# Token sums on GpSimd instead of TensorE, two more row buffers, and a changed first and last step in a two-part attention kernel

## The chip, the cores and the metric

The kernel runs on one core of one Trainium2 chip. The metric is the device time of one execution in microseconds, as the median of several runs.

## The reference

Two attention blocks work on separate inputs of 2048 tokens and 640 features, with 32 heads of 20 features each; their outputs stand side by side in one array of 2048 x 1280, in bf16.

```python
def _A_ref(x, wqkv, wo):          # H = 32, Dh = 20, W = 256
    q, k, v = split_heads(x @ wqkv)
    scores = einsum("bhqd,bhkd->bhqk", q, k) * Dh ** -0.5
    mask = (i - j >= 0) & (i - j < W)
    p = softmax(where(mask, scores, -1e9))
    return heads_joined(einsum("bhqk,bhkd->bhqd", p, v)) @ wo

def _B_ref(x, wqkv, wo):
    q, k, v = split_heads(x @ wqkv)
    phi = lambda t: where(t > 0, t + 1, exp(t)) + 1e-6
    pq, pk = phi(q), phi(k)
    kv = einsum("bhsd,bhse->bhde", pk, v)
    z = einsum("bhsd->bhd", pk)                       # sum over all tokens
    num = einsum("bhqd,bhde->bhqe", pq, kv)
    den = einsum("bhqd,bhd->bhq", pq, z)[..., None] + 1e-6
    return heads_joined(num / den) @ wo
```

A is sliding-window attention, B is linear attention. The vector z, the sum of the keys' features over the tokens, is what the change works on most.

## The kernel before

The tokens are worked in four tiles of 512 (t = 0 to 3), of four blocks of 128 rows each. One function, `build`, first lists operations: each has its engine or engines, its dependencies, and the buffers that it takes and gives back. The order in which they are then written out is a fixed list, `SEQ`: each number is an operation times eight plus an engine, so the list also says which of ScalarE (ACT) and VectorE (DVE) makes an eviction. Every engine executes its own instructions strictly in this order, and so do the queues of DMA issues on SP, ACT and POOL. Where an engine has to wait, all that is behind it on that engine waits too.

Part A. `proj` makes q and k of a tile (line 577), and `proj_v` makes v (line 638). Heads that lie badly for TensorE's row groups are moved to another tile, `odd`, by DMAs issued on POOL (lines 608 and 611), called relays here. `attn` makes scores in one PSUM buffer S (line 708), ACT takes the exponentials (line 724), DVE multiplies the window's edges by 0 or 1 (line 736, the masks, a product of two inputs in SBUF), and TensorE multiplies p by v (line 764). `a_out` divides and multiplies by the output weights (line 798).

Part B. `b_keys` makes pk = phi(k) for all 16 blocks of rows (line 913; ACT and DVE finish it in lines 874 to 881); pk of a tile of 512 tokens lies in SBUF under the tags K0 to K3. `b_sums` makes G, the product of B's input and pk over all tokens (line 938). `b_z` sums pk over the tokens: 32 matmuls with a matrix of ones (line 974) into two PSUM buffers, which DVE splits into a bf16 part and its rest (lines 986 and 989, z.hi and z.lo), ten matmuls with one column that turn the sum into a column (line 995), and on DVE the block pattern Zc (line 1002). `b_kvwo` multiplies G by the value weights and the output weights (lines 1037 and 1055). `b_query` makes pq (line 1107) and the denominators (line 1125), divides (line 1171), and multiplies by the matrix of `b_kvwo` (line 798 again).

`finish_rows` makes one block of 128 output rows: two groups of five matmuls of 320 columns each, an eviction of each into a row buffer (`osb`, lines 484 on ACT and 486 on DVE), and one store of the row (line 812). The row buffers are four slots, O0 to O3:

```python
pl = Planner(FB + ["S0"] + [f"O{i}" for i in range(PRM.get("nosb", 4))] + ["L0"])
```

A slot is taken by the first eviction of a row and given back when the store has landed. The products of line 1055 are evicted into the same slots.

PSUM for all but the scores is four buffers, F0 to F3. At the start PE runs matmuls on a tile of zeros, `warm`, that DVE fills first (line 504, matmuls of line 1185); x of the first 128-row blocks is loaded, turned by TensorE (line 1242) and copied out; and the value weights arrive in five blocks of 128 rows, three on ACT's queue and two on SP's.

Of the kernel before, what the change touches and what calls it, by code (L numbers as in the profile page):

```python
# [14 lines left out]
PRM = {"sq": "SP", "dens": 4}  # L15
TUNE = {}
SEQ = [
# [372 lines left out]
def build(nc, pools, A_x, A_wqkv, A_wo, B_x, B_wqkv, B_wo, out):  # L390
# [6 lines left out]
    NQ = 512  # L397
    NTT = 4
    HALF = 320
    WIDE = bool(PRM.get("wide"))  # L400
    SWD = 640 if WIDE else 512
    scale = float(Dh) ** -0.5
    NF = 3 if WIDE else 4
# [1079 lines left out]
```

## Time and profile before

| | us |
|---|---|
| median of 3 runs | 250.51 (250.25 to 251.5) |
| the profiled execution, its own time | 250.49 |
| its span, first to last instruction | 248.8 |
| PE busy | 239.9 |
| ACT busy | 200.8 |
| DVE busy | 172.6 |
| POOL busy | 40.4 |

The span is one execution's time from the first to the last instruction; the execution's own time also holds what lies around it. PE is TensorE's matmuls, PEld its weight loads, DVE VectorE, ACT ScalarE, POOL GpSimd, SP SyncE. In a row of a group, the numbers behind the bars are busy us, mean ns of one, and idle us of the engine before it with what ended the idle time. In the chain and the timeline a row starts with its start and its length in us.

### The profile page before, as it was taken

What the parts mean: (1) busy time and instruction counts of PE and PEld (TensorE: products, weight loads), DVE (VectorE), ACT (ScalarE), POOL (GpSimd) and SP (SyncE); (2) the same over time, 40 slices, a digit from 0 to 9 for tenths busy, and PEclk for the clock granted to TensorE, in tenths of its full rate; (3) what the DMA queues carried; (4) which work ended last, traced back from release to release, by engine and by line L of the source; (5) the groups of instructions that cost most, each with busy time, mean ns of one, the idle gap of its engine ahead of it and who ended that gap; (6) DMA issues with size and microseconds to landing.
All of it is one profiled execution on the core that took longest, in us unless ns stands there. A gap on an engine that the chain in (4) does not pass through costs nothing.

```text
span 248.8 us, 9643 instructions
## 1 busy us (share of the span) xinstructions
PE 239.9 (96%) x4167; PEld 144.3 (58%) x4193; DVE 172.6 (69%) x441; ACT 200.8 (81%) x222; POOL 40.4 (16%) x93
## 2 busy tenths in 40 slices
PE   7999999999999999999999999999989999999993
PEld 6644565454655666545566666666555665565671
DVE  2553587778679978886666363369999899949740
ACT  2459898988999999988998788789999987946532
POOL 6003460063002601004078000000000000000000
PEclk9999999999999999999999999999999999999999
DMA  6999226649364759913573768863545472236433
GB/s 216 284 148 243 59 66 148 154 90 166 87 223 111 198 99 213 277 42 72 143 194 75 124 154 258 202 164 105 159 139 151 119 167 84 76 114 186 135 128 111
DMA packets 54216, 36.61 MB, mean 147 GB/s; under 512 B 34249, under 2 KB 52761, under 8 KB 54169
## 3 DMA queue, kind: packets, MB, share of 16 engines
q1 hardware_dynamic: 50537, 31.52, 49.7%
q0 software_dynamic: 2048, 2.63, 5.3%
q10 hardware_dynamic: 1584, 1.80, 2.2%
q8 instruction: 33, 0.54, 1.0%
q14 instruction: 14, 0.11, 0.2%
HBM read 13.90 MB, written 10.26 MB: 97 GB/s over the span
## 4 chain that ended last, share of the span: by engine, by line
PE 87%; ACT 6%; DVE 3%; issue 2%; DMA 1%; ACTq 0%; DVEq 0%
PE F L577 17%; PE F L798 16%; PE S L708 10%; PE F L638 9%; PE F L913 9%; PE F L938 9%; PE F L764 6%; PE F L1107 5%; ACT p L724 4%; DMA out_dram<-osb 1%; PE F L1185 1%; DVE pq L881 1%; PE F L1037 1%; ACT e L874 1%; PE F L1242 1%
## 5 line engine op out<-in xcount | busy, mean ns | idle before, releaser
L724 ACT ACTIVATE p<-S 128x2048 bf16<-128x2048 f32 x76 | 141.1, 1856 | 16.4 <-PE S L708 14.5
L736 DVE TENSOR_TENSOR p<-p,strip 128x256 bf16<-128x256 bf16 (+2 forms) x140 | 49.4, 381 | 21.1 <-ACT p L724 20.5
L874 ACT ACTIVATE e<-F 128x320 bf16<-128x320 f32 (+1 forms) x52 | 25.5, 501 | 8.3 <-PE F L1107 5.8
L638 PE MATMUL F<-wv,xT 128*128 128x320 bf16 x160 | 31.7, 300 | 0.1
L913 PE MATMUL F<-wkB,xT 128*128 128x320 bf16 x160 | 30.7, 299 | 0.2 <-issue 0.2
L798 PE MATMUL F<-woA,oc 128*128 128x320 bf16 x160 | 30.3, 300 | 0.0
L611 POOL DMA_DIRECT2D odd<-st x32 | 18.2, 573 | 69.3 <-ACT st L484 28.8
L577 PE MATMUL F<-xT,wk 128*128 128x512 bf16 x91 | 27.8, 380 | 0.3
L577 PE MATMUL F<-xT,wq 128*128 128x512 bf16 x92 | 26.9, 380 | 0.5 <-issue 0.3
L938 PE MATMUL F<-pk,xtok 128*128 128x320 bf16 x160 | 27.1, 300 | 0.0
L798 PE MATMUL F<-kvwo,pq 128*128 128x320 bf16 x160 | 25.9, 300 | 0.9 <-DVE pq L1171 0.4
L1107 PE MATMUL F<-xT,wqB 128*128 128x512 bf16 x91 | 25.4, 381 | 0.3
L486 DVE CAST ost<-F 128x512 bf16<-128x512 f32 x26 | 17.1, 685 | 10.2 <-PE F L764 10.0
L486 DVE CAST even<-F 128x512 bf16<-128x512 f32 x24 | 16.5, 688 | 8.2 <-PE F L577 7.9
L486 DVE CAST osb<-F 128x320 bf16<-128x320 f32 x33 | 15.5, 486 | 8.6 <-PE F L798 7.9
L608 POOL DMA_DIRECT2D odd<-even x32 | 16.6, 524 | 25.4 <-DVE even L486 23.2
L764 PE MATMUL F<-p,vt 64*32 64x320 bf16 (+4 forms) x720 | 20.5, 253 | 0.0
L638 PEld LDWEIGHTS <-xT 128*128 128x128 bf16 x160 | 15.1, 98 | 9.2 <-issue 1.3
L913 PEld LDWEIGHTS <-xT 128*128 128x128 bf16 x160 | 15.0, 98 | 8.9 <-issue 1.2
L764 PE MATMUL F<-p,sw 64*32 64x320 bf16 (+3 forms) x720 | 19.9, 253 | 0.2 <-DVE kvs L486 0.2
L798 PEld LDWEIGHTS <-pq 128*128 128x128 bf16 x160 | 14.9, 98 | 8.7 <-issue 1.6
L484 ACT CAST osb<-F 128x320 bf16<-128x320 f32 x31 | 12.6, 426 | 8.5 <-PE F L798 6.2
(85 smaller groups left out, 295.8 us busy)
## 6 DMA issues: line engine op xcount, KB each, us to landing
OD<-ost SPq DMA_DIRECT2D x32, 128.0 KB, 2.2
out_dram<-osb SPq DMA_DIRECT2D x24, 160.0 KB, 2.1
oc<-OD SPq DMA_DIRECT2D x4, 640.0 KB, 4.9
xtok<-in_B_x_dram SPq DMA_DIRECT2D x4, 640.0 KB, 4.5
odd<-even POOLq DMA_DIRECT2D x32, 48.0 KB, 2.9
sw<-vt SPq DMA_DIRECT2D x16, 87.0 KB, 3.1
out_dram<-osb ACTq DMA_DIRECT2D x8, 160.0 KB, 2.1
odd<-st POOLq DMA_DIRECT2D x32, 32.0 KB, 3.1
```

Source lines behind the costliest of these rows:

```text
L486: nc.vector.tensor_copy(out=dst, in_=src)
L577: nc.tensor.matmul(ps[:, a:b], lhsT=w[:, kt, i, :], rhs=xb["t"][:, kt, a:b], start=(kt == 0), stop=(kt == KT - 1))
L638: return lambda ps: nc.tensor.matmul(ps[:], lhsT=xb["t"][:, kt, bb * P : bb * P + P], rhs=rhs_(), start=(kt == 0), stop=(kt == KT - 1))
L708: nc.tensor.matmul(st["s"][64 * i : 64 * i + 64, o0 : o0 + b - a], lhsT=kb["t"][32 * j : 32 * j + Dh, sl, ko : ko + 64], rhs=qb["t"][32 * ...
L724: nc.scalar.activation(out=o_, in_=i_, func=ACT.Exp, scale=scale)
L736: nc.vector.tensor_tensor(out=x, in0=x, in1=mkv[:, None, :].to_broadcast([P, 4, 64 * w]), op=ALU.mult)
L764: nc.tensor.matmul(O[i][32 * j : 32 * j + 32, a:b], lhsT=lhsT, rhs=pb["t"][64 * i : 64 * i + 64, o0 + js * j : o0 + js * j + b - a], start ...
L798: return lambda ps: nc.tensor.matmul(ps[:], lhsT=lhs(c), rhs=rhs(c, hf), start=(c == 0), stop=(c == KT - 1))
L874: nc.scalar.activation(out=eb["t"][:, 0:n], in_=ps[:], func=ACT.Exp)
L913: return lambda ps: nc.tensor.matmul(ps[:], lhsT=xb["t"][:, kt, b * P : (b + 1) * P], rhs=R["wkB"][:, kt, hf * HALF : (hf + 1) * HALF], st ...
L938: return lambda ps: nc.tensor.matmul(ps[:], lhsT=R["xt", tb // 4][:, tb % 4, c * P : (c + 1) * P], rhs=R["pk", tb // 4][:, tb % 4, hf * HA ...
L1107: return lambda ps: nc.tensor.matmul(ps[:], lhsT=R["wqB"][:, kt, :].rearrange("p (f c) -> p c f", c=KT)[:, c, :], rhs=xb["t"][:, kt, :], s ...
```

## The change

- The sums of line 974 go. Fifteen GpSimd additions of 128 x 640 sum the 16 blocks of pk into a float32 tile, `zacc`. What follows (z.hi, z.lo) reads this tile instead of PSUM, in one instruction of 640 columns each instead of two of 320. The ten one-column matmuls then take a column of ones.
- Two more row slots, OK2 and OK3, lie over pk of tiles 2 and 3. They are held from the start and given free by z.hi and z.lo, when pk is no longer needed.
- The last block of rows of B (`ob3.3`) is made in three groups, of 320, 160 and 160 columns, and stored in two parts, of 480 and 160 columns.
- The warm-up matmuls read a constant of ones that the framework fills ahead of all engines' work, and there are 22 instead of 20 (beside 8 others that are the same in both).
- Block 0 of the value weights is the first, not the second, on ACT's queue. This and all else that is only order comes with a new list `SEQ`, which also gives some evictions to the other engine.
- Six rounds of four matmuls of 8 columns stand ahead of the first denominator. In the first tile, p times v goes through its pieces in another order.

In the new order the additions stand on POOL behind twelve of the sixteen relays of the last tile and ahead of the other four. The last group of all is one of 160 columns (columns 320 to 480), evicted by ACT, and the store of 480 columns, issued by ACT, is the last.

The diff, without `SEQ` and without paths that the settings leave off:

```diff
-PRM = {"sq": "SP", "dens": 4}
+PRM = {"sq": "SP", "dens": 4, "zs": "POOL", "xo": 1, "dpad": 6, "lastb": 3, "nwarm": 22}
...
+    XO = {"OK2": "K2", "OK3": "K3"} if PRM.get("xo", 1) else {}
+    pl = Planner(FB + ["S0"] + list(XO) + [f"O{i}" for i in range(PRM.get("nosb", 4))] + ["L0"])
+    held = [{} for _ in XO]
+    for g_ in held:
+        pl.op({"SP": 1}, lambda e: None, -(10 ** 8), [], name="hold", slots=(1, "O"), g=g_)
...
-        warm = mk("o", [P, NQ], BF16, "warm", tag="L0")
-        nc.vector.memset(warm[:], 0.0)
+        warm = nc.const_aps.tensor(1.0, (P, P), BF16)
...
+    def row_tile(sb, name):
+        tag = sb["slot"][0]
+        return mk("over", [P, D], BF16, name, tag=XO[tag]) if tag in XO else mk("o", [P, D], BF16, name, tag="osb" + tag)
+
-    def finish_rows(tb, col0, lhs, rhs, key, deps, name):
+    def finish_rows(tb, col0, lhs, rhs, key, deps, name, last=False):
...
-        for hf in range(2):
+        cuts = [(0, HALF), (HALF, 480), (480, D)] if last else [(0, HALF), (HALF, D)]
+        for k, (a, b) in enumerate(cuts):
...
-        st = dma(lambda e: q_of(e).dma_start(out=out2[tb * P : (tb + 1) * P, col0 : col0 + D], in_=sb["t"][:]), D_STORE, -4000, ends, name="store")
+        for a, b, need in [(0, 480, ends[:2]), (480, D, ends[2:])] if last else [(0, D, ends)]:
+            st = dma(lambda e, a=a, b=b: q_of(e).dma_start(out=out2[tb * P : (tb + 1) * P, col0 + a : col0 + b], in_=sb["t"][:, a:b]), (340, 1, int(420 * (b - a) / D), 350), -4000, need, name="store")
...
+            for k in range(1, NT):
+
+                def add(e, k=k):
+                    if "zacc" not in R:
+                        R["zacc"] = mk("const", [P, D], F32, "zacc")
+                    blk = lambda i: R["pk", i // 4][:, i % 4, :]
+                    (nc.vector if ZS == "DVE" else nc.gpsimd).tensor_tensor(out=R["zacc"][:], in0=blk(0) if k == 1 else R["zacc"][:], in1=blk(k), op=ALU.add)
+
+                need = pk_ops[2 * k : 2 * k + 2] + (pk_ops[0:2] if k == 1 else [prev])
+                prev = pl.op({ZS: {"DVE": 820, "POOL": 1500}[ZS]}, add, 4000 + k, need, name=f"zs{k}")
...
+            a = pl.op({"DVE": 490 if one else dve_ps(HALF)}, hi, EVK, need, name="z.hi", rel=[(g_, 0) for g_ in (held[0:1] if one else held[k : k + 1])])
+            evs.append(pl.op({"DVE": 820 if one else dve_ps(HALF)}, lo, EVK, [a], name="z.lo", rel=rel + [(g_, 0) for g_ in (held[1:2] if one else [])]))
...
+                for i in range(PRM.get("dpad", 0) if t == 0 else 0):
+                    for s_ in range(4):
+                        nc.tensor.matmul(dg["w"][32 * s_ : 32 * s_ + 32, 256:264], lhsT=ones[:], rhs=ones[:, 0:8], start=True, stop=True, tile_position=(0, 32 * s_), skip_group_check=True)
...
-                nc.tensor.matmul(psum(g)[:, 0:P], lhsT=warm[:, 0:P], rhs=warm[:, 0:P], start=True, stop=True)
+                nc.tensor.matmul(psum(g)[:, 0:P], lhsT=warm[:, 0:P], rhs=warm, start=True, stop=True)
```

More of the change, by code (lines that the diff above doesn't have):

```diff
@@ L502, in build @@
     if not dry:
-        warm = mk("o", [P, NQ], BF16, "warm", tag="L0")
-        nc.vector.memset(warm[:], 0.0)
-        nc.scalar.preload_act_table_set("natural_log_exp_and_others")
+        warm = nc.const_aps.tensor(1.0, (P, P), BF16)
+        if not XT0:
+            nc.scalar.preload_act_table_set("natural_log_exp_and_others")
         tiny = mk("const", [P, 1], F32, "tiny")
         nc.vector.memset(tiny[:], 1e-6)
-        tinyo = mk("const", [P, 1], F32, "tinyo")
-        nc.scalar.activation(out=tinyo[:], in_=tiny[:], func=ACT.Exp)
+        if not XT0:
+            tinyo = mk("const", [P, 1], F32, "tinyo")
+            nc.scalar.activation(out=tinyo[:], in_=tiny[:], func=ACT.Exp)
         ident = mk("const", [P, P], BF16, "ident")
@@ L576, in m @@
                     w = wq if which == "q" else wk
-                    nc.tensor.matmul(ps[:, a:b], lhsT=w[:, kt, i, :], rhs=xb["t"][:, kt, a:b], start=(kt == 0), stop=(kt == KT - 1))
+                    rhs = xb["t"][:, :, kt, :] if t == 0 and XT0 else xb["t"][:, kt, a:b]
+                    nc.tensor.matmul(ps[:, a:b], lhsT=w[:, kt, i, :], rhs=rhs, start=(kt == 0), stop=(kt == KT - 1))
                 return m
@@ L637, in mm @@
                         rhs_ = lambda: wv[:, kt, :].rearrange("p (a i n) -> p a i n", a=2, i=2)[:, :, i, :]
+                        if t == 0 and XT0:
+                            return lambda ps: nc.tensor.matmul(ps[:], lhsT=xb["t"][:, bb, kt, :], rhs=rhs_(), start=(kt == 0), stop=(kt == KT - 1))
                         return lambda ps: nc.tensor.matmul(ps[:], lhsT=xb["t"][:, kt, bb * P : bb * P + P], rhs=rhs_(), start=(kt == 0), stop=(kt == KT - 1))
@@ L966, in b_z @@
         R["cst"] = co
-        zg = {}
-        def emz(e):
-            ps = [psum(zg, hf, [P, HALF]) for hf in range(2)]
-            for b in range(4):
-                for hf in range(2):
-                    for s in range(4):
-                        nc.tensor.matmul(ps[hf][32 * s : 32 * s + 32, :], lhsT=ones[:], rhs=R["pk", s][:, b, hf * HALF : (hf + 1) * HALF], start=(b == 0), stop=(b == 3), tile_position=(0, 32 * s), skip_group_check=True)
         R["gm"] = gm = list(g_mm)
-        zo = pl.op({"PE": 1120}, emz, kv("z", key), [pk_ops, gm], mode="z", slots=(2, "F"), g=zg, name="z", cls="Z", ni=64)
@@ L978, in b_z, with emz @@
         hl = {}
+        ZS = PRM.get("zs", "PE")
+        if ZS == "PE":
+            zg = {}
+            def emz(e):
+                ps = [psum(zg, hf, [P, HALF]) for hf in range(2)]
+                for b in range(4):
+                    for hf in range(2):
+                        for s in range(4):
+                            nc.tensor.matmul(ps[hf][32 * s : 32 * s + 32, :], lhsT=ones[:], rhs=R["pk", s][:, b, hf * HALF : (hf + 1) * HALF], start=(b == 0), stop=(b == 3), tile_position=(0, 32 * s), skip_group_check=True)
+            zo = pl.op({"PE": 1120}, emz, kv("z", key), [pk_ops, gm], mode="z", slots=(2, "F"), g=zg, name="z", cls="Z", ni=64)
+            g_mm.append(zo)
+            parts = [(psum, (zg, hf), slice(hf * HALF, (hf + 1) * HALF), [zo, gm], [(zg, hf)]) for hf in range(2)]
+        else:
+            prev = None
+            for k in range(1, NT):
[6 more added lines that the diff above has]
+                prev = pl.op({ZS: {"DVE": 820, "POOL": 1500}[ZS]}, add, 4000 + k, need, name=f"zs{k}")
+                g_mm.append(prev)
+            parts = [(lambda: R["zacc"], (), slice(0, D), [prev, gm], [])]
@@ L1011, in ldv @@
             R["wvB"] = mk("w", [P, KT, D], BF16, "wvB", tag="wv")
[L1012 removed]
+            for a, b in WSP:
+                nc.sync.dma_start(out=R["wvB"][:, a:b, :], in_=wBv[:, a:b, 2 * D : 3 * D])
         wvB_op = dma(ldv, D_WFULL, lk, [R["mm", "v", 3]], name="ld.wvB", earliest=130)
@@ L1090, in em @@
             R["wqB"] = mk("w", [P, KT, D], BF16, "wqB", tag="wq")
-            nc.sync.dma_start(out=R["wqB"][:], in_=wBv[:, :, 0:D])
+            for a, b in WSP:
+                nc.sync.dma_start(out=R["wqB"][:, a:b, :], in_=wBv[:, a:b, 0:D])
         R["wq_op"] = dma(em, D_WFULL, key, [R["mm", "q", 3]], name="ld.wqB", earliest=140)
@@ L1184, in em @@
             for i in range(n):
-                nc.tensor.matmul(psum(g)[:, 0:P], lhsT=warm[:, 0:P], rhs=warm[:, 0:P], start=True, stop=True)
-        pl.op({"PE": n * 54}, em, key, [], slots=(1, "F"), g=g, rel=[(g, 0)], name="warm", ni=2 * n)
-    heat(nwarm, -(10 ** 8))
+                nc.tensor.matmul(psum(g)[:, 0:P], lhsT=warm[:, 0:P], rhs=warm, start=True, stop=True)
+            for i in range(pad):
+                for s_ in range(4):
+                    nc.tensor.matmul(psum(g)[32 * s_ : 32 * s_ + 32, 0:32], lhsT=warm[:, 0:32], rhs=warm[:, 0:32], start=True, stop=True, tile_position=(0, 32 * s_), skip_group_check=True)
+        pl.op({"PE": n * 54 + pad * 14 + (95 if pad else 0)}, em, key, [], slots=(1, "F"), g=g, rel=[(g, 0)], name="warm", ni=2 * n + 8 * pad)
+    heat(nwarm, -(10 ** 8), PRM.get("pad", 0))
     for i in range(PRM.get("nfill", 4)):
         heat(2, 10 ** 7 + i)
-    pl.free["PE"] = 1450
+    pl.free["PE"] = 1060
     pl.free["SP"] = 1040
-    pl.free["ACTQ"] = 1500
-    pl.free["ACT"] = 2400
+    pl.free["ACTQ"] = 1040 if XT0 else 1500
+    pl.free["ACT"] = 3500 if XT0 else 2400
     pl.net = 2140
@@ L1203, in build, with x0_tile, em, tables @@
     x0l = []
-    for b in range(4):
-        def em(e, b=b):
-            if "t" not in x0n:
-                x0n["t"] = mk("o", [P, 4, D], BF16, "x0n", tag="oc0")
-            nc.sync.dma_start(out=x0n["t"][:, b, :], in_=xA[b * P : (b + 1) * P, :])
-        x0l.append(dma(em, D_XROW, (-1000, -999, -994, -993)[b], [], name=f"x0n{b}"))
-    oc_r.boxes.append({"users": x0n_users, "tag": "oc0"})
+    def x0_tile():
+        if "t" not in x0:
+            x0["t"] = mk("x", [P, 4, KT, P] if XT0 else [P, KT, NQ], BF16, "xT", tag="x0")
+        return x0["t"]
+    if XT0:
+        for b, n in ((0, 1), (1, 1), (2, 2))[0 if XT0 == 1 else 2 :]:
+            def em(e, b=b, n=n):
+                for i in range(b, b + n):
+                    nc.sync.dma_start_transpose(out=x0_tile()[:, i, :, :], in_=xA[i * P : (i + 1) * P, :])
+            o = dma(em, (720, n, 700, 900), (-1000, -999, -994)[b], [], name=f"x0T{b}")
+            x0late = x0.setdefault("late", []) + [o] * n
+            x0["late"] = x0late
+        def tables(e):
+            nc.scalar.preload_act_table_set("natural_log_exp_and_others")
+            tinyo = mk("const", [P, 1], F32, "tinyo")
+            nc.scalar.activation(out=tinyo[:], in_=tiny[:], func=ACT.Exp)
+        pl.op({"ACT": 1600}, tables, -(10 ** 6), [], name="tables")
+    if XT0 != 1:
+        for b in range(2 if XT0 else 4):
+            def em(e, b=b):
+                if "t" not in x0n:
+                    x0n["t"] = mk("o", [P, 4, D], BF16, "x0n", tag="oc0")
+                q_of(e).dma_start(out=x0n["t"][:, b, :], in_=xA[b * P : (b + 1) * P, :])
+            x0l.append(dma(em, D_XROW, (-1000, -999, -994, -993)[b], [], name=f"x0n{b}", eng="ACTQ" if XT0 and b else "SP"))
+        oc_r.boxes.append({"users": x0n_users, "tag": "oc0"})
     for kt in range(KT):
-        load_w("SP" if kt in (1, 3) else "ACTQ", f"wv{kt}", lambda kt=kt: wv[:, kt, :], lambda kt=kt: wAv[:, kt, 2 * D : 3 * D], D_XROW, -998 + kt)
+        load_w("SP" if kt in PRM.get("wvsp", (1, 3)) else "ACTQ", f"wv{kt}", lambda kt=kt: wv[:, kt, :], lambda kt=kt: wAv[:, kt, 2 * D : 3 * D], D_XROW, -998 + kt)
     for kt in range(KT):
@@ L1237, in build @@
             W["c" + which].append(o)
-    for b in range(4):
+    for b in range((4, 0, 2)[XT0]):
         def tr(c, b=b):
@@ L1251, in build @@
         x0n_users.append(g["mm"])
+    x0["ready"] += x0.get("late", [])
     def em_wk(e):
         R["wkB"] = mk("w", [P, KT, D], BF16, "wkB", tag="wB")
-        nc.sync.dma_start(out=R["wkB"][:], in_=wBv[:, :, D : 2 * D])
+        for a, b in WSP:
+            nc.sync.dma_start(out=R["wkB"][:, a:b, :], in_=wBv[:, a:b, D : 2 * D])
     proj(0, "q", [-100, -99, -80, -79, -76], 1)
```

81 lines of the change are left out of this document (41 added, 40 removed), and 187 rows, old and new, of the table SEQ.

## The prediction

> **What bounds the kernel now.** I read the page's first parts, then PE's waits, then the chain, and last busy time by stretches.
>
> ```profile
> span 248.8 us, 9643 instructions
> PE 239.9 (96%) x4167; PEld 144.3 (58%) x4193; DVE 172.6 (69%) x441; ACT 200.8 (81%) x222; POOL 40.4 (16%) x93
> PE 87%; ACT 6%; DVE 3%; issue 2%; DMA 1%; ACTq 0%; DVEq 0%
> ```
>
> PE is busy for 96% of the span and makes 87% of the chain that ended last. Its waits are few; each row has the total, how often, and the longest:
>
> ```profile
> PE F L1185 <- DVE tiny L507: 1.5, 1, 1.5
> PE S L708 <- ACT p L724: 0.5, 1, 0.5
> PE F L798 <- ACT osb L484: 0.4, 1, 0.4
> ```
>
> So the time can fall by work that leaves PE, by the 1.5 us ahead of PE's first matmul, by the few waits, or by what lies behind PE's last matmul. One stretch is different. Here are span, then busy time of PE, PEld, DVE, ACT and POOL:
>
> ```profile
> 132.00:140.00 8.00, 8.00 (x120) 5.00 (x119) 4.55 (x14) 6.66 (x7) 4.21 (x11) 1.00 0.65 108
> 140.00:150.00 10.00, 9.94 (x229) 6.70 (x214) 5.41 (x14) 8.27 (x7) 0.00 (x0) 1.00 0.49 115
> 150.00:160.00 10.00, 10.00 (x229) 6.48 (x228) 2.47 (x6) 7.88 (x7) 0.00 (x0) 1.00 0.94 249
> 166.00:175.00 9.00, 8.80 (x171) 5.69 (x167) 7.82 (x21) 8.00 (x8) 0.00 (x0) 1.00 0.35 104
> 175.00:188.00 13.00, 11.89 (x253) 7.07 (x254) 12.38 (x31) 12.85 (x15) 0.00 (x0) 1.00 0.45 139
> ```
>
> From 175 to 188 us ACT is busy for 12.85 of 13 and PE loses 1.1: there ACT and DVE set the pace. From 132 to 160 PE is full, while DVE is busy for 12.4 of 28 and POOL is free after 136.5.
>
> **Token sums to GpSimd.** The 32 matmuls of line 974 go; fifteen GpSimd additions of 640 columns come.
>
> ```profile
> 165.08 0.79 PE F L938 x5
> 166.30 1.20 PE F L974 x32
> 186.33 0.41 PE F L1125 x20
> ```
>
> PE loses 1.20 us of work that stands on the chain. The order of the changed program is laid out anew, but PE changes its kind of work 178 times in both, so I book no change in switching. Of the sums' followers, four DVE instructions of 320 columns become two of 640, and the ten matmuls with one column stay. The new order must not be late: the DVE queue has the first follower behind G's last copies, so the additions are due when G ends, at 165.9 us here. They stand in POOL's queue behind twelve relays of the last tile's q and k, whose like run here from 124.04; twelve at 0.51 to 0.59 us make 130.5, and the last ends at 136.5. I take a start of 132.
>
> ```profile
> 124.04 0.51 POOL L608 DMA_DIRECT2D odd<-even  x1 [8.25 <-DVE even L486]
> 135.32 1.18 POOL L611 DMA_DIRECT2D odd<-st  x2
> L512 POOL TENSOR_SCALAR_AFFINE_SELECT ident<-ident 128x128 bf16<-128x128 bf16 x1 | 0.3, 287 | 0.1
> L956 POOL TENSOR_SCALAR_AFFINE_SELECT blk<-blk 128x128 bf16<-128x128 bf16 x1 | 0.5, 529 | 0.1
> ```
>
> No row shows a GpSimd addition. The nearest GpSimd rows read and write 128 columns in 287 and 529 ns; five times the columns is 1.4 to 2.6 us, 22 to 40 us for fifteen. I take the low end, 1.5 us each, since an addition has a plain pattern, like the shorter row: 22.5 us, done at 154.5, 11 us before it is due. Break-even is (165.9 - 132) / 15 = 2.3 us each. [...]
>
> Four relays stand behind the additions. Their readers are scores of the last tile's odd heads, behind the first denominator (186.33), so they may be 20 us later than here at no cost.
>
> What the additions do to DVE is the doubtful part. Two pairs of mask products, the first beside GpSimd instructions, the second alone:
>
> ```profile
> 134.38 0.60 DVE L736 TENSOR_TENSOR p<-p,strip 128x256 bf16<-128x256 bf16 x2 [1.42 <-ACT p L724]
> 144.73 0.50 DVE L736 TENSOR_TENSOR p<-p,strip 128x256 bf16<-128x256 bf16 x2 [0.87 <-ACT p L724]
> 150.83 0.42 DVE L736 TENSOR_TENSOR p<-p,strip 128x512 bf16<-128x512 bf16 x1
> 153.37 1.26 PE F L764 x92
> 132.00:140.00 8.00, 2.67 (x8) 1.00 0.65 108
> 140.00:150.00 10.00, 2.84 (x8) 1.00 0.49 115
> 150.00:160.00 10.00, 1.27 (x3) 1.00 0.94 249
> ```
>
> The last three rows are line 736 alone: 19 products in the additions' 28 us. Beside a 0.32 us GpSimd instruction a pair took 0.10 us more. At that price, 19 x 0.1 = 1.9 us, it vanishes in DVE's 15.6 idle us. Behind the products stand DVE's evictions, and p times v on PE waits for both; the last mask of one group ended at 151.25, 2.1 us before its matmuls began. Bounds: nothing, to 3.3 us (worked out with the rivals). I take 0.3.
>
> **Two more row buffers, and the last rows.** The chain at the end:
>
> ```profile
> 231.11 5.54 PE F L798 x40
> 239.88 0.43 ACT osb L484
> 240.34 3.43 DMA out_dram<-osb
> 243.84 0.43 ACT osb L484
> 244.32 0.85 PE F L798 x5
> 245.20 0.42 ACT osb L484
> ```
>
> Two groups of the page beside it, the first for DVE's evictions, the second for what a column costs on ACT:
>
> ```profile
> L486 DVE CAST osb<-F 128x320 bf16<-128x320 f32 x33 | 15.5, 486 | 8.6 <-PE F L798 7.9 <-ACT osb L484 0.5
> L724 ACT ACTIVATE p<-S 128x2048 bf16<-128x2048 f32 x76 | 141.1, 1856 | 16.4 <-PE S L708 14.5
> ```
>
> A row's store has to land (3.43 us) before an eviction finds a row buffer, and PE's last five matmuls wait for that eviction: 0.40 us. With six buffers, freed at the sums' followers long before, the eviction of 243.84 needs no landing. What is late next is PE's own stream, 5.54 / 40 = 0.14 us a matmul and 0.69 a group, against evictions of 0.42 on ACT and 0.49 on DVE in parallel: PE stays first. Gain 0.40, at worst nothing, if another buffer is late. The last group shrinks from 320 to 160 columns: at no more than 1856 / 2048 = 0.9 ns a column its eviction on ACT is up to 0.14 us shorter, and I take 0.13 less behind the last matmul. The matmul columns are the same, in five more instructions; nothing is booked. The last store holds 480 columns, not 640, and the 160-column store is issued before it on the other queue. I book both landings as equal.
>
> The same buffers serve the K-V-output product (line 1055), where PE lost 1.1 us in the last stretch above. ACT limits that stretch, but less DVE work ahead of it, and no wait for buffers, may give some back: 0 to 1.1, I take 0.4.
>
> **Start, padding.** The warm-up reads a constant that exists before the engines start, so PE begins some 0.4 us earlier; the first weight block is issued first on its queue instead of second.
>
> ```profile
> 1.50 0.86 ACTq L542 DMA_DIRECT2D wv<-in_A_wqkv_dram  x2
> 4.03 1.41 PE L1242 MATMUL F<-ident,x0n 128*128 128x128 bf16 x10
> 4.81 0.49 DVE L486 COPY xT<-F 128x640 bf16<-128x640 bf16 x1 [3.36 <-PE F L1242]
> 5.66 2.47 PE L638 MATMUL F<-wv,xT 128*128 128x320 bf16 x16
> 7.97 0.44 PE L1242 MATMUL F<-ident,x0n 128*128 128x128 bf16 x5
> ```
>
> The transposes cannot move much: they need rows of x that are issued as before. The first of them is copied out by 5.30, yet the first real matmul starts at 5.66, so at most 0.36 us goes there. PE also runs slow at first (ten transposes in 1.41 us, later five in 0.44); if its speed follows the time since its first matmul, full speed comes 0.4 us earlier and a few matmuls gain 0.1 each. The changed first copy is on ACT, at 0.9 ns a column some 0.6 us instead of 0.49. I take 0.2 of 0 to 0.5, since weights and their copies could be late next.
>
> Six rounds of four 8-column matmuls come before the first denominator. Its own rounds stand among the 0.41 us above for five; these are shorter, so 6 x 0.08 = 0.5 at most, and at least 6 x 4 x 3.5 ns, the spacing within a round, 0.08. The ten one-column matmuls are the nearest row:
>
> ```profile
> L995 PE MATMUL F<-c,hl 128*128 128x1 bf16 x10 | 0.5, 177 | 0.0
> ```
>
> That is 0.05 each; with loads four to a round, 6 x 0.03 = 0.2 (an estimate). The changed order of p times v in the first tile keeps the same columns: nothing.
>
> **Sum.** -1.20 (sums) - 0.40 - 0.13 (end) - 0.4 (product stage) - 0.2 (start) + 0.2 (padding) + 0.3 (DVE) = -1.83. The profiled execution took 250.49 us, 1.7 of it outside its span of 248.8, and the median of the three runs is 250.51: 248.7.
>
> **Rivals.** (1) *DVE and GpSimd shut each other out.* If a product with both inputs in SBUF cannot run during an addition, each addition stops DVE once, for nearly all of it: 15 x 1.4 = 21 us against 15.6 idle ones. DVE falls 5.4 us behind, 2.1 of that are the masks' lead, so PE waits 3.3: 248.4 without my 0.3, plus 3.3, is 251.7. It decides from 15.6 + 2.1 = 17.7 us of blocking, 1.2 us per addition. For it: every group of exponentials is followed by one to four products. Against: the pair above paid only 0.10. [...]
>
> (2) *ACT takes the gain.* If the stage from 166 to 188 is set by exponentials, what PE saves before it is given back: the sums' 1.20, the start's 0.2 and the stage's 0.4 are gone, and 0.53 at the end stays, less 0.2: 250.2, no change. For it: 12.85 of 13. Against: in the nine us before, ACT has 1.0 idle to take the work earlier.
>
> (3) *The additions are late.* At 2.6 us each they end at 132 + 39.7 = 171.7; DVE stands behind them from 165.9, and PE runs out of buffers within a group: 5 us, so 253.7. Then the change does not take the sums off the path at all.
>
> **How the numbers follow.** Forecast 0.64, rival 2 0.18, rival 1 0.13, rival 3 0.05. The lower end has the best values: end 0.53, stage 1.1, start 0.5, padding 0.08, DVE 0: -3.25, 247.2; the new order may close some of the other short waits, so 246.9. The upper end holds rival 1's 251.7. Within 0.5%, about what a measurement can tell from no change, is 249.26 to 251.76: rival 2, and 0.02 of the forecast with 0.05 of rival 1 (which grows with the length of an addition): same 0.25. Slower takes the longer half of rival 1 and rival 3: 0.13. Faster 0.62.
>
> **What would show it.** Right: no line like 974 on PE; fifteen additions on POOL of about 1.5 us that end before G does; mask products near 0.28 to 0.55 us; no wait of PE for an osb eviction; first projection matmul near 5.4 us. Wrong: mask products or gaps on DVE of over 1 us between 132 and 165, PE waiting for p in that time (rival 1); DVE's first follower waiting for POOL (rival 3); the first denominator at 186 as before (rival 2).

## The result and the profile after

The changed kernel took 257.69 us in the median of six runs (256.56 to 258.93), the kernel before 250.57 in the same comparison: ratio 1.0268, 95% interval 1.0245 to 1.0291. (Here and below the ratio comes from all the runs, and is not the quotient of the two medians.) It is 7 us slower, where I had forecast 1.8 us less; 257.7 also lies outside my range. The profiled execution took 256.56 us, the fastest of the six; what the slower five did beyond it no trace shows. Of the runs below, one of the kernel with long gaps, of 261.55 us, fell in a slower state of the chip, and its median is that of the other three. The lines of the profiled execution's page that answer to those of before:

```profile
span 255.1 us, 9682 instructions
PE 243.3 (95%) x4192; PEld 144.5 (57%) x4192; DVE 185.4 (73%) x442; ACT 200.5 (79%) x219; POOL 63.8 (25%) x108
PE 81%; DVE 9%; DMA 4%; ACT 2%; SPq 2%; issue 1%; ACTq 0%; DVEq 0%
```

DVE is 12.8 us busier than before, with 442 instructions for 441, and its share of the chain went from 3% to 9%. PE's longest waits:

```profile
PE F L815 <- DVE oc L878: 3.7, 1, 3.7
PE F L815 <- DVE GT L493: 1.2, 1, 1.2
```

Neither wait was there before, and the 0.4 us for `osb` is gone. (`oc` is part A's divided output, which the output weights multiply; GT is a piece of G, whose eviction frees a PSUM buffer.) Busy time by stretches (span, then PE, PEld, DVE, ACT, POOL, then PE's granted clock):

```profile
132.00:140.00 8.00, 4.32 (x39) 2.35 (x40) 7.35 (x8) 3.72 (x3) 7.69 (x5) 0.90 0.73 177
140.00:150.00 10.00, 10.00 (x200) 6.22 (x198) 7.93 (x12) 7.31 (x8) 9.45 (x8) 0.91 0.27 76
150.00:160.00 10.00, 8.81 (x124) 5.41 (x124) 6.71 (x11) 7.09 (x7) 6.69 (x7) 1.00 0.81 187
138.00:140.00 2.00, 2.00 (x24) 1.04 (x24) 1.35 (x3) 1.84 (x2) 1.92 (x2) 0.61 1.29 282
140.00:142.00 2.00, 2.00 (x10) 1.12 (x8) 1.78 (x3) 0.42 (x1) 1.84 (x3) 0.54 0.76 202
```

In the first stretch PE was busy for 4.32 of 8 us; before, for all 8. Behind that pause its clock was at half speed, as the last two rows show (the trace has 0.5 for 3.41 us, from 138.44). The chain there (start and length in us):

```profile
129.90 0.49 DVE vt L493
130.39 3.22 DVE p L747 x2
133.61 3.61 DVE oc L878 x3
137.27 0.85 PE F L815 x5
```

The timeline's row of the additions, all but the first:

```profile
131.99 22.74 POOL L1009 TENSOR_TENSOR zacc<-zacc,pk 128x640 f32<-128x640 f32 x14
```

Five products, which by before's rows take some 2.3 us together, took 6.8 us while the additions ran. Grouped by shape, from 130 to 155 us, first before, then after:

```profile
L736 DVE TENSOR_TENSOR p<-p,strip 128x256 bf16<-128x256 bf16 x8 | 2.2, 299 | 3.1 <-ACT p L724 3.1
L736 DVE TENSOR_TENSOR p<-p,strip 128x512 bf16<-128x512 bf16 x6 | 2.4, 419 | 0.4 <-ACT p L724 0.4
L736 DVE TENSOR_TENSOR p<-p,strip 128x768 bf16<-128x768 bf16 x4 | 2.2, 552 | 0.0
L860 DVE TENSOR_TENSOR oc<-oc,recA 128x640 bf16<-128x640 bf16 x4 | 1.9, 485 | 0.0
L850 DVE TENSOR_SCALAR_CACHE_REDUCE junk<-osum 128x512 bf16<-128x512 bf16 x1 | 0.7, 672 | 0.0
```

```profile
L747 DVE TENSOR_TENSOR p<-p,strip 128x256 bf16<-128x256 bf16 x5 | 6.9, 1374 | 0.0
L747 DVE TENSOR_TENSOR p<-p,strip 128x512 bf16<-128x512 bf16 x4 | 4.1, 1013 | 0.0
L878 DVE TENSOR_TENSOR oc<-oc,recA 128x640 bf16<-128x640 bf16 x4 | 4.2, 1077 | 0.0
L747 DVE TENSOR_TENSOR p<-p,strip 128x768 bf16<-128x768 bf16 x3 | 3.9, 1297 | 0.7 <-ACT p L735 0.7
L868 DVE TENSOR_SCALAR_CACHE_REDUCE junk<-osum 128x512 bf16<-128x512 bf16 x1 | 0.7, 672 | 0.0
L493 DVE CAST GT<-F 128x320 bf16<-128x320 f32 x3 | 1.4, 482 | 0.9 <-PE F L956 0.9
```

Only the products with both inputs in SBUF became longer. A DVE instruction with one SBUF input (672 ns in both) and evictions from PSUM (482 ns; 486 before) did not. The 16 products took 19.1 us; at before's prices it would be 6.8. So 12.3 us were lost.

Comparing the starts of the 76 exponentials of both traces shows where the 6.25 us of span arose. Just ahead of the first wait the changed kernel is 0.42 us early; PE's pause makes it 3.44 late, the half clock 4.97, the second wait 6.33. It then falls back to 5.89 ahead of the place of TensorE's sums and to 5.54 past it; the last exponential is 5.46 late, and from there to the end another 0.79 are lost.

### The profile page after: what moved, and what is told of

Its sections match the earlier page's. It is cut to its first block, busy times and chain, and to the rows that moved or that the text cites. A ratio compares the mean times of both kernels' runs of the same rounds, so it can differ in the third digit from the quotient of the medians.

```text
span 255.1 us, 9682 instructions
## 1 busy us (share of the span) xinstructions
PE 243.3 (95%) x4192; PEld 144.5 (57%) x4192; DVE 185.4 (73%) x442; ACT 200.5 (79%) x219; POOL 63.8 (25%) x108
## 4 chain that ended last, share of the span: by engine, by line
PE 81%; DVE 9%; DMA 4%; ACT 2%; SPq 2%; issue 1%; ACTq 0%; DVEq 0%
PE F L815 17%; PE F L586 16%; PE S L719 9%; PE F L931 8%; PE F L956 7%; PE F L649 7%; PE F L776 6%; PE F L1146 6%; DVE p L747 2%; DMA woA<-in_A_wo_dram 2%; DVE oc L878 2%; DVE pq L899 2%; DMA x0n<-in_A_x_dram 1%; DVE kvs L493 1%; SPq L1352 1%
## 5 line engine op out<-in xcount | busy, mean ns | idle before, releaser
L747 DVE TENSOR_TENSOR p<-p,strip 128x256 bf16<-128x256 bf16 (+2 forms) x140 | 59.1, 452 | 15.9 <-ACT p L735 15.5
L815 PE MATMUL F<-woA,oc 128*128 128x320 bf16 x160 | 32.0, 304 | 4.9 <-DVE oc L878 3.7
L586 PE MATMUL F<-xT,wq 128*128 128x512 bf16 x100 | 28.8, 380 | 0.1
L1146 PE MATMUL F<-xT,wqB 128*128 128x512 bf16 x100 | 26.9, 380 | 0.6 <-DVE pq L899 0.5
L815 PE MATMUL F<-kvwo,pq 128*128 128x320 bf16 (+1 forms) x165 | 26.1, 296 | 0.0
L491 ACT CAST osb<-F 128x320 bf16<-128x320 f32 (+1 forms) x28 | 11.5, 415 | 16.7 <-PE F L815 16.6
L493 DVE CAST osb<-F 128x320 bf16<-128x320 f32 x37 | 17.3, 484 | 7.7 <-PE F L815 6.3
L815 PEld LDWEIGHTS <-oc 128*128 128x128 bf16 x160 | 14.9, 99 | 14.0 <-DVE oc L878 4.3
L1009 POOL TENSOR_TENSOR zacc<-zacc,pk 128x640 f32<-128x640 f32 x14 | 21.7, 1551 | 1.1
L931 PEld LDWEIGHTS <-xT 128*128 128x128 bf16 x160 | 15.1, 98 | 9.6 <-issue 1.1
```

Source lines behind the costliest of these rows:

```text
L493: nc.vector.tensor_copy(out=dst, in_=src)
L586: nc.tensor.matmul(ps[:, a:b], lhsT=w[:, kt, i, :], rhs=rhs, start=(kt == 0), stop=(kt == KT - 1))
L747: nc.vector.tensor_tensor(out=x, in0=x, in1=mkv[:, None, :].to_broadcast([P, 4, 64 * w]), op=ALU.mult)
L815: return lambda ps: nc.tensor.matmul(ps[:], lhsT=lhs(c), rhs=rhs(c, a, b), start=(c == 0), stop=(c == KT - 1))
L931: return lambda ps: nc.tensor.matmul(ps[:], lhsT=xb["t"][:, kt, b * P : (b + 1) * P], rhs=R["wkB"][:, kt, hf * HALF : (hf + 1) * HALF], st ...
L1146: return lambda ps: nc.tensor.matmul(ps[:], lhsT=R["wqB"][:, kt, :].rearrange("p (f c) -> p c f", c=KT)[:, c, :], rhs=xb["t"][:, kt, :], s ...
```

## The experiments

The theory behind them, from the groups above (products of 256 columns took 1374 ns beside the additions and 299 before): a DVE product with two SBUF inputs cannot run during a GpSimd instruction that reads SBUF. What each theory and rival would give stands in each expectation. Behind each expectation come the median, in brackets the ratio to the kernel before, measured in the same comparison, and its 95% interval. The diffs leave `SEQ` out.

### The token sums back on TensorE

```diff
-PRM = {..., "zs": "POOL", ...}
+PRM = {..., "zs": "PE", ...}
```

> The changed kernel with the 32 matmuls of the token sums back on PE; all else, the order too, as changed. Theory A (an addition on GpSimd and a DVE product of two SBUF inputs exclude each other, DVE falls behind, PE waits 3.85 and 1.36 us and then runs at half clock for 3.4 us): both waits and the half clock go, 1.2 us of matmuls come back; the exponentials stay 0.3 to 0.5 us ahead of the kernel before as they are until 132 us, the end keeps its extra us: 250.5 to 251.5 us, mask products of 256 columns at 0.28. Theory B (the new order or the other parts make the loss): stays at 256 to 258.

252.0 us beside 250.70 (ratio 1.0058, 1.0038 to 1.0077). This is 0.5 us above theory A's range and far under B's. No long PE wait, products as before. So 5.7 of the 7 us come with the additions, TensorE's 1.2 already set against them. The rest of the change costs 1.3, where I had forecast a gain of 0.9; in the profiled run the exponentials are some 0.5 us late from the first tile on, and 0.87 are lost behind the last of them.

### Only the additions, in the order of before

```diff
-PRM = {..., "xo": 1, "dpad": 6, "lastb": 3, "nwarm": 22}
+PRM = {..., "xo": 0, "dpad": 0, "lastb": -1, "nwarm": 20}
```

> The kernel before, in its own order, with only the token sums as fifteen GpSimd additions behind the same relays (and the constant warm-up operand): no new row buffers, no split last block, no padding. Theory A: DVE and PE stall as in the changed kernel, 4 to 7 us less 1.2 for the matmuls that went: 253.5 to 257. Theory B: at or under the kernel before, 249 to 250.5.

254.76 us (1.0172, 1.0123 to 1.0222). The same loss with other neighbours. PE's longest waits were 0.8 to 1.4 us, and its clock stayed at 1.0. It is 2.9 us below the changed kernel: 1.3 are the rest of the change (above), and 1.6 are near the 1.5 that the half clock cost behind the long pause (a subtraction; no run shows the two apart).

### The additions spread from 45 to 138 us

> The changed kernel with fourteen of the fifteen additions moved forward in POOL's queue, behind the block of keys that each needs (two at about 45 us, four at 56 to 76, four at 82 to 95, three at 102 to 113, one at 114), the last one left at 130. Same work, same order on all other engines. Theory A: each addition still stops at most one product for up to 1.5 us, but never several in a row, so the two long PE waits go: 249 to 252. Theory B or a cost of GpSimd's additions as such: 256 to 258.

255.63 us (1.0188, 1.0145 to 1.0231). Fourteen of the fifteen additions were put ahead in POOL's queue to just behind the pk blocks that they add. The loss moved with them: PE waited for DVE's pk for 2.9 us in four pieces and for `st` for 1.1, most of it between 77 and 100 us. DVE has less idle time there (before, it is busy for 58.28 of the 73 us from 45 to 118, and for 12.43 of 28 from 132 to 160), so spreading helps little; 252 was too low.

### GpSimd as busy, but reading nothing

```diff
-                    (nc.vector if ZS == "DVE" else nc.gpsimd).tensor_tensor(out=R["zacc"][:], in0=..., in1=blk(k), op=ALU.add)
+                    nc.gpsimd.memset(R["zacc"][:], 1.0)
+                    nc.gpsimd.memset(R["zacc"][:], 1.0)
```

The sums are not formed.

> The changed kernel with each addition replaced by two GpSimd memsets of the same 640 columns: POOL's queue is held for about as long (some 20 us) and writes as much, but reads nothing from SBUF. It leaves out the token sums, so B's output is not the reference's. Theory A in its narrow form (only a GpSimd instruction that reads SBUF excludes the products): no long PE wait, mask products at 0.28 us, 249 to 251. Rival C (a busy POOL queue delays the four relays behind it, or GpSimd's writes are enough): waits as in the changed kernel, 255 to 258.

250.18 us (0.9979, 0.9952 to 1.0006). Here are GpSimd's and the products' groups:

```profile
L1011 POOL MEMSET zacc<- 128x640 f32 x15 | 9.5, 633 | 0.8
L749 DVE TENSOR_TENSOR p<-p,strip 128x256 bf16<-128x256 bf16 x68 | 18.7, 286 | 14.0 <-ACT p L737 13.8
```

Two times 9.5 us of GpSimd, in the same place of its queue and writing twice the columns, and no product is longer. Neither the busy queue, nor the four relays behind it, nor the writes cost anything: the reads do. This kernel also shows what the rest of the change is worth without the reads: 0.5 us less than before, by an interval that still holds no change at all.

### One SBUF input on GpSimd instead of two

```diff
+                    nc.gpsimd.tensor_copy(out=R["zacc"][:], in_=blk(k))
```

> The changed kernel, with each addition replaced by a GpSimd copy of the same 128 x 640 block of pk into the float32 tile: one SBUF input, the same output. The sum is not formed, so B's half of the output is not the reference's. Theory A (any GpSimd read of SBUF holds VectorE's two-input products): longer masks and a PE wait again; a copy of 0.7 to 1.5 us gives 15 times that, 10 to 22 us of blocking, so 251.5 to 257 us. Theory B (only a GpSimd instruction with two SBUF inputs does): as with memsets, 250.2 us, masks of 286 / 419 / 550 ns.

251.78 us (1.0038, 1.0017 to 1.0060). The group of the copies, and PE's longest wait:

```profile
L1011 POOL CAST zacc<-pk 128x640 f32<-128x640 bf16 x15 | 12.6, 837 | 0.9
```

```profile
PE F L817 <- DVE oc L880: 0.9, 1, 0.9
```

One read is enough: products of 640 columns took up to 997 ns in place of 484. The loss is less than with additions; a copy is 0.84 us and not 1.55.

### Additions in quarters

```diff
+                    for c0 in range(0, D, 160):
+                        cq = slice(c0, c0 + 160)
+                        nc.gpsimd.tensor_tensor(out=R["zacc"][:, cq], in0=(blk(0) if k == 1 else R["zacc"])[:, cq], in1=blk(k)[:, cq], op=ALU.add)
```

> The changed kernel, with each addition cut into four of 160 columns: 60 GpSimd instructions for 15, the same columns read in all. Theory A (a VectorE product with two SBUF inputs is held until the GpSimd instruction under way has ended): a piece is near 1551 / 4 = 390 ns, up to 0.5 us with a fixed part, and a product waits for one piece, not for a whole addition. Some 30 products by 0.2 to 0.5 us are 6 to 15 us, inside VectorE's 15.6 idle us: 251 to 254 us, the longest PE wait under 1.5 us. Theory B (the two share the reads, so what counts is the columns read in all): as the changed kernel, 256 to 259 us, PE waits of 3 to 4 us.

251.32 us (1.0014, 0.9997 to 1.0030): 6 us less than with whole additions, at the lower edge of A's 251 to 254. Two groups, from 130 to 162 us:

```profile
L1013 POOL TENSOR_TENSOR zacc<-zacc,pk 128x160 f32<-128x160 f32 x56 | 28.5, 541 | 0.0
L749 DVE TENSOR_TENSOR p<-p,strip 128x256 bf16<-128x256 bf16 x9 | 4.0, 441 | 4.2 <-ACT p L737 4.1
```

GpSimd reads the same columns and is busy for longer (30.8 us with the first four, for 23.1), yet no product took over 0.84 us. Here what counts is how long one product is held, not how much GpSimd reads.

### Halves, and three attempts to see why

```diff
-                    for c0 in range(0, D, 160):
+                    for c0 in range(0, D, HALF):
```

> The changed kernel, with each addition in two halves of 320 columns (30 GpSimd instructions). Between 541 ns of a piece of 160 columns (251.3 us) and 1551 of a whole one (257.7 us) a half should take 0.85 to 0.95 us. Theory A (the length of one GpSimd instruction decides, and the loss begins where VectorE's products stand in a row and use up its idle time): 251.5 to 253.5 us, the longest PE wait 1 to 2 us, products of 640 columns held to 0.8 to 0.95 us. Rival (the number of columns read decides, and quarters escape by another cause): 256 us or more.

274.01 us (1.0899, 1.0846 to 1.0951). Neither theory had this. The group of the additions, the row of one product in the timeline, and PE's wait:

```profile
L1013 POOL TENSOR_TENSOR zacc<-zacc,pk 128x320 f32<-128x320 f32 x28 | 20.9, 779 | 0.0
```

```profile
132.14 21.80 DVE L749 TENSOR_TENSOR p<-p,strip 128x256 bf16<-128x256 bf16 x1 [0.65 <-ACT p L737]
```

```profile
PE F L817 <- DVE oc L880: 20.9, 1, 20.9
```

One product of 256 columns waited through the whole row of additions. It was not held for one GpSimd instruction (0.78 us): it ended at 153.94 us, the last addition at 153.79, and between two halves it did not get in. So the length of one instruction (my theory for the quarters) is not the rule.

A small memset, which reads nothing, behind each half:

```diff
+                        nc.gpsimd.memset(R["zpad"][:], 0.0)      # 128 x 8
```

> The changed kernel with each addition in two halves of 320 columns, as in the run of 274.0 us, and behind each half a GpSimd memset of 128 x 8 into a tile that nothing reads. The memset reads no SBUF. Theory A (VectorE's product of 256 columns waited 21.8 us because the next half took the inputs before VectorE could; an instruction between them that reads nothing lets it in): the product waits for one half, 0.8 us, no wait of 20 us, 251.5 to 254 us. Theory B (the additions hold the inputs from the first to the last of the row, whatever lies between, until GpSimd turns to a relay): one product held for 22 us and more again, 274 to 278 us.

273.20 us (1.0900, 1.0861 to 1.0939): theory A fell here too. Four products got in, each behind one half, then one did not. The memsets' group, and the product in the timeline (two in one row; the second, of 512 columns, took 19.97 us):

```profile
L1016 POOL MEMSET zpad<- 128x8 f32 x30 | 2.9, 95 | 0.0
```

```profile
135.11 20.77 DVE L749 TENSOR_TENSOR p<-p,strip 128x256 bf16<-128x256 bf16 x2
```

Five such memsets behind each half, about 0.65 us between two halves:

> The changed kernel with each addition in two halves of 320 columns and five small GpSimd memsets (128 x 8, about 60 ns from start to start) behind each half: some 300 ns between two halves in which GpSimd reads nothing, for 60 to 95 ns in the run of 273.2 us. Theory A (VectorE looks again at times of its own, and a short gap can lie between two looks; a longer one is always met): no product held for more than a half, 0.8 us, and 251.5 to 254 us. Theory B (the gap has no part in it; a product that lost its turn is not looked at before the additions end): one hold of 20 us and more, 275 to 285 us, since the row of additions grows by 6 us.

258.91 us (1.0360, 1.0300 to 1.0420), between the two theories. No product was held for longer than a half now (1.08 us at most, its own time included): every product met one of the long gaps. The time went elsewhere, since the row of additions now ended at 173.6 us. DVE's timeline there, and PE's wait:

```profile
173.62 0.52 DVE L1030 CAST hl<-zacc 128x640 bf16<-128x640 f32 x1 [5.91 <-POOL zpad L1017]
```

```profile
PE F L1083 <- DVE pq L901: 4.6, 1, 4.6
```

That is the lateness of my third rival, made by hand: DVE stands 5.9 us behind the sums, PE 4.6.

Pieces of 480 and 160 columns, no gap:

```diff
+                    for c0, c1 in [(0, 480), (480, D)]:
```

> The changed kernel with each addition in two pieces of 480 and 160 columns, no gap: about 1.1 and 0.48 us, 30 GpSimd instructions as with halves. Theory A (the even row of halves, one start each 745 ns, happens to miss VectorE's looks; another spacing does not): no product held longer than two pieces, 1.6 us, 251.5 to 256 us. Theory B (what starves is 30 short additions in a row, whatever their spacing): one hold of 20 us, 270 us or more.

263.07 us (1.0470, 1.0426 to 1.0514), between the two theories. Two rows of DVE's timeline:

```profile
139.71 3.36 DVE L749 TENSOR_TENSOR p<-p,strip 128x256 bf16<-128x256 bf16 x2
150.26 6.09 DVE L749 TENSOR_TENSOR p<-p,strip 128x256 bf16<-128x256 bf16 x1
```

Most products took 1.3 to 1.9 us, about one pair of pieces, and one 6.1 us, through eight pieces to the end of the row. The turn is missed again and again, but not always: it came only behind a piece of 480 columns. The pieces of 160 behind them took 0.53 to 0.80 us where a product got in and 0.48 where none did, while those of 480 took 1.08 to 1.10 throughout.

### Whole additions with a small memset

> The changed kernel, with the whole additions of 640 columns and the same small memset behind each. Theory A (in the changed kernel each product waits for one addition already, since the two take turns; the gap adds no turn, only the length of one addition decides): masks and PE waits as in the changed kernel, 255.5 to 258 us. Theory B (some products of the changed kernel wait for more than one addition, and the gap ends that): fewer and shorter PE waits, under 254 us.

257.99 us (1.0317, 1.0291 to 1.0343), as A had it, and the trace repeats the changed kernel's row by row (three products of 640 columns in 3.68 us, PE's wait 3.7). With whole additions a product got in at the next border already, and paid up to one addition (1.55 us) each time.

### The last rows in one store

```diff
-PRM = {..., "zs": "POOL", "xo": 1, "dpad": 6, "lastb": 3, ...}
+PRM = {..., "zs": "PE", "xo": 1, "dpad": 6, "lastb": -1, ...}
```

> The changed kernel with the token sums on TensorE and the last block of rows in two groups of 320 columns and one store, as before the change; the rest of the changed order stays. Theory A (the split last store and its issue on SP behind two others cost the 0.9 us at the end): 251.0 to 251.3 us, span minus PE's last matmul back near 3.6 us. Theory B (the end is late by the changed order, the split has no part in it): 252.0 us, as with the token sums on TensorE alone.

251.75 us (1.0042, 1.0025 to 1.0059). From PE's last matmul to the end of the span it is 4.63 us, 4.75 with the split, 3.65 before. The split is not the cause of the longer end; the median is still between the two theories.

### The additions on DVE, and the row buffers by themselves

Both in the order of before. First the sums as additions on DVE, in its idle stretches from 138 us, with the row buffers:

```diff
+PRM = {..., "zs": "DVE", "xo": 1, "dpad": 0, "lastb": -1, "nwarm": 20}
```

> The kernel before in its own order, with the warm-up from a constant, the two row buffers more, and the fifteen additions of 128 x 640 on VectorE, put into its idle stretches from 138 to 165 us (13.4 idle us there by the trace of before); GpSimd gets none, the last block of rows is not split. Theory A (the change lost by GpSimd's reads, and 1.2 us of TensorE's sums are to be had where VectorE is idle): 15 x 0.7 to 0.8 us = 11 to 12 us fit, minus 1.2 for the sums, minus 0.4 for the last row buffer, plus 0.2 for the start: 249.1 to 250.3 us. Rival (VectorE's idle time is waiting that others need, so its evictions come late): PE waits for evictions of 1 us or more between 138 and 166 us, 250.5 to 253 us.

250.54 us beside 250.92 (0.9974, 0.9951 to 0.9997). That is just above A's range, and the rival's waits are not there: the additions take 822 ns each, and no wait of PE shows between 130 and 166 us. But the 1.2 us are not had. Their group, and a row of PE's timeline with the wait ahead of it:

```profile
L1011 DVE TENSOR_TENSOR zacc<-zacc,pk 128x640 f32<-128x640 f32 x14 | 11.5, 822 | 0.2
```

```profile
168.63 0.43 PE L721 MATMUL S<-even 20*64 20x320 bf16 x24 [0.79 <-ACT p L737]
```

Of 1.20 us the next exponentials start only 0.40 earlier, and PE waits 0.79 us for ACT that it did not before: there ACT takes the gain. The 0.40 is lost again too: the last exponential starts 1.04 us later than before (0.40 in the same kernel without the row buffers, below), and why is open. Then the row buffers alone, sums on TensorE (`"zs": "PE"`):

> The kernel before in its own order, with the token sums on TensorE, and two of the changes: the two row buffers more and the warm-up from a constant. Theory A (what the last row buffer's wait costs is had back): PE's last matmul 0.4 us earlier behind the last exponential, 250.3 us beside 250.7 for before. Theory B (what PE gains the stores give back, since they then land closer to one another: 3.2 us lie between the last eviction and the end of the span in before, 3.7 to 4.4 in every kernel without that wait): 250.5 to 250.9 us, the wait gone and the landing 0.4 us longer.

250.30 us beside 250.99 (0.9971, 0.9950 to 0.9992), as A had it: PE's last matmul ends 30.37 us behind the start of the last exponential, 30.93 before. Last, the additions on DVE without the row buffers (`"xo": 0`):

> The kernel before in its own order, with the token sums as fifteen additions on VectorE in its idle stretches, and without the two row buffers. Theory A (the rows' gain is had as well as the sums'): 0.4 us more than with the rows, near 250.9 us. Theory B (the rows bring nothing at the end): as with them, 250.5 us; the 0.33 us that TensorE's sums gave after 166 us and the 1.0 us that was lost again before the last exponential show here too.

250.59 us (0.9982, 0.9953 to 1.0011). The wait at the end is gone here too, though the last row takes the same slot, O0, as in before: from the last exponential to PE's last matmul it is 30.36 us, with the buffers or without. The landing of a store differs from one to the next: the 3.43 us in the chain of before are a slow one beside the median of its page (the last number, in us):

```profile
out_dram<-osb SPq DMA_DIRECT2D x24, 160.0 KB, 2.1
```

So the wait that I booked was an accident of one execution's landings, as far as these traces show, and the two buffers are worth less than I thought. These three kernels can't be told apart, and by the ratio none gains more than 0.3%.

## Why the prediction was wrong

**DVE beside the additions: +0.3 forecast, the step that failed.** "Beside a 0.32 us GpSimd instruction a pair took 0.10 us more. At that price, 19 x 0.1 = 1.9 us, it vanishes in DVE's 15.6 idle us." Both halves are wrong. The price came from a neighbour of 0.32 us and was kept for one of 1.5 us; 16 products lost 12.3 us, 0.77 each. And a sum of idle time over 28 us is no cover for a loss that comes in a row: 12.3 is less than 15.6, yet the five products from 130.39, two masks and three of `oc`, lost 4.5 us between them, and PE, which needed the third `oc`, stood for 3.7. The lead there was some 0.9 us (an estimate, from the two numbers), not the 2.1 that I had read from one group of masks. In place of 0.3 us the runs show 6.75 at the exponentials: the two waits and the half clock.

**Rival 1 had the mechanism and 0.13; its 251.7 was too low.** It set 21 us of blocking against idle time and got 3.3 us of waiting, for p. Measured are 12.3 us of blocking, under its own limit of 17.7, and still PE waited, for `oc` and GT: 3.86 and 1.36 us late at the two waits, and 1.53 by the half clock in between, which I had in no case. The traces show who is touched (two SBUF inputs against a GpSimd read, 1374 ns for 299; not against memsets, 286), and put an end to my 0.10 as evidence against it. No run shows the 1.4 us per addition that this rival counted, which was an estimate: a product lost 0.77 us in the mean beside whole additions, and between halves one was held through 28 of them, for 21.80 us.

**The other terms: -2.13 together, -0.5 measured.** Without the reads, with memsets, the changed kernel took 250.18 us beside 250.70. So 248.7 would not have come without the interference either. That 250.18 is the second rival's 250.2 is luck: this rival lost the sums' gain and kept that of the end, while with memsets the last exponential starts 0.86 us sooner than before and the end gives 0.50 of it back.

**Additions: right.** 1.55 us each for 1.5, from 130.5 to 154.7 for 132 to 154.5; DVE's first follower did not wait for them. Their relays cost nothing.

**TensorE's sums: -1.20 forecast.** In the changed order all of it is had: past the sums' place, from one exponential to the next, the kernel with the sums on TensorE falls back by 0.94 us against before, the one with memsets gains 0.35, 1.29 apart; so the new order by itself loses 0.94 there. In the order of before the second rival's limit shows, and 0.40 is left.

**End: -0.53 forecast, +0.79 measured.** The wait is gone, but PE's last matmul comes only 0.22 us sooner behind the last exponential (30.71 us for 30.93). The last eviction takes 0.29 for 0.42 us, as booked, but what follows grew. The chain's last row, and the last evictions and the last store in the timeline:

```profile
242.81 7.60 PE F L815 x60
```

```profile
247.84 1.85 DVE L493 CAST osb<-F 128x320 bf16<-128x320 f32 x4 [0.41 <-PE F L815]
249.75 0.98 ACT L491 CAST osb<-F 128x320 bf16<-128x320 f32 x3 [3.65 <-PE F L815]
250.76 0.34 ACTq L830 DMA_DIRECT2D out_dram<-osb  x1
```

From the last eviction's end (250.73) to the end of the span are 4.33 us, 3.19 before. "I book both landings as equal" failed. The twelve kernels with the changed order have 4.35 to 4.81 us behind PE's last matmul, the five with that of before 3.65 to 4.38. The profile of before, at 3.65, is the shortest of all, so part of the 0.79 may be that one execution's luck. Why is open; more stores close to the end is an argument, and not shown.

**K-V-output stage (line 1055): -0.4 forecast, little seen and nothing kept.** With memsets the lead of the exponentials is 0.93 us at the stage's start (174.4 in before), 1.24 at most within it, 1.07 behind it (189.9), and 0.86 at the last exponential.

**Start: -0.2, had at first and not kept; padding: +0.2, about right.** In the twelve profiles with that start the first projection matmul comes 0.20 to 0.58 us sooner than before (5.08 to 5.46 us for 5.66). But the second tile's first exponential lies 0.49 us earlier to 0.73 later, so what is left of the gain can't be read from one profile. The padding was not tried by itself; in the changed kernel's trace its first matmul starts 0.15 us ahead of the first denominator's (191.53 and 191.68).

## What to carry to other kernels

Before work moves to an idle GpSimd, list DVE's instructions with two SBUF inputs that will run beside it: here such a product waited for up to a whole GpSimd addition (1.55 us), or through many halves of one (28, 21.80 us); of the GpSimd instructions tried here only memsets, which read no SBUF, were free (250.18 us beside 250.70). Set such a loss against the idle time between two waits of the bound engine, not against a sum over the stretch. The price taken beside a neighbour of 0.32 us, 0.10 us for a pair, did not hold beside one of 1.55, where each product lost 0.77.

## What the runs showed of the hardware

- Between two GpSimd instructions DVE gets its turn or misses it: between whole additions (1.55 us) and between quarters (0.54) it had it at the next border each time, between halves (0.78) not for 20 us, with a memset of 95 ns behind each half four times and then not for 20 us, with gaps of 0.65 us always, and with pieces of 480 and 160 columns only behind those of 480. A gap between the records does not decide alone: whole additions lie 78 to 79 ns apart, while the records of quarters and of halves both overlap by some 32, and quarters let DVE in. What decides is not settled; the looks at times of DVE's own, which two of the expectations suppose, are shown by no run.
- Behind long pauses PE's clock was at half speed. In the changed kernel it stood at 0.5 for 3.41 us behind the pause of 3.7 us, and its mean over the execution was 0.992, for 0.999 before. With the pause of 20.9 us, between halves, it was 0.63 in the mean from 134 to 153 us, within the pause already, 0.50 from 153 to 156 and 0.56 from 156 to 160, and 0.962 over the execution; with the pause of 19.0 us, a memset behind each half, 0.961. With a pause of 3.7 us (whole additions with a memset) the mean was 0.993, with one of 4.6 us (long gaps) 0.982, with two, of 5.2 and 3.3 us (pieces of 480 and 160 columns), 0.977. The eleven kernels without a pause of over 1.4 us between matmuls, that of before among them, had 0.995 to 1.0, and of the pauses none between 1.4 and 3.3 us was seen. The wait of 3.7 us in the changed kernel thus cost 5.4 (3.86 and 1.53 at the exponentials).
